# ScalarE's order in the step of a group's votes: q's scaling, slices and y's planes ahead of the first exponential

## The chip, the cores and the metric

The kernel runs on one core of a Trainium2 chip. The metric is the device time of one launch in microseconds; the time shown for the kernel before is the median of three runs. One more run was recorded by the hardware profiler, and all rows of the trace below come from that one. TensorE is PE here, VectorE DVE, ScalarE ACT, GpSimd POOL; SP is the engine that issues most DMAs.

## The reference

Attention over pooled keys, and then a mixture of experts that picks one expert for each row. Four batches, 12288 query rows each, 128 columns; 768 pooled keys per batch; 8 experts with 1024 hidden columns.

```python
kv_flat = kv.reshape(B, H//4, 4, W//4, 4, C).mean(axis=(2, 4)).reshape(B, -1, C) @ w_sr
k = v = kv_flat
a = softmax(q @ k.T / sqrt(C))            # per row, over 768 keys
x = a @ v                                 # 49152 rows of 128
logits = x @ w_gate                       # 8 experts
e = argmax(logits);  g = softmax(logits)[e]
y = g * (relu(x @ w1[e]) @ w2[e])
```

## The kernel before

The rows are taken in 96 blocks of 512 rows. A block is worked on in four chunks of 128 rows for its scores. fp32 products are made of three fp16 matmuls: every operand is cut into a high half and a low half (what the high half leaves), and high x high, high x low and low x high are summed. So each matmul operand costs one instruction that makes its high half and one that makes its low half.

The main loop has one step for each block t from 8 on. A step holds work of several blocks side by side:

- the scores of block t, chunk by chunk: six matmuls into a PSUM buffer `s` (there are two, used in turn), the row maximum on VectorE (L369, then L371 turns it into the bias `nmax`), the exponential on ScalarE into `a` (L376), its high half `ah[:, 0]` (chunks 0 and 2 on ScalarE, L399; chunks 1 and 3 on GpSimd, L397), its low half on GpSimd (L401), and a transposing DMA of both halves into `aT` (L402). `a`, `ah` and `nmax` have three buffers each, used in turn by the chunks;
- the product of `aT` with the values for block t-2 (18 matmuls into one PSUM bank `m`), its halves xh (ScalarE, L412) and xl (VectorE, L417), and its logits;
- the expert's two products for block t-8: eight slices f = 0 to 7, each three matmuls into a bank `m`, the slice's high half hh (ScalarE, L518) and low half hl (VectorE, L524), and then three matmuls into `y`. The second product runs three slices behind the first, so slices 5, 6 and 7 of a block go into `y` at the start of the next step. `y` has one PSUM buffer: slice 0 of the next block can go into it only when ScalarE has copied it out, as two planes of 16-bit halves (y's planes, `y_planes`, L547, two copies). There are three banks `m`, shared by the slices and the product with the values;
- block t+1's q: scaled on ScalarE (q_apply, L599), transposed on VectorE (q_turn, L603), high half on ScalarE (q_high, L607), low half on GpSimd (q_low, L612); the bound of block t+2's q on VectorE (q_max, L582). `q_scale` makes the unit that q_apply needs (L148, L149, L328);
- block t-9's output: planes joined and scaled on GpSimd (L553, L557), written by a DMA.

Four blocks form a group (two, in two places of the first batch). After a group's last block has its logits, the group votes on the expert that is computed for it; rows that chose another expert are done at the end. The votes take VectorE first: six small operations on the group's logits (`gate_part`, L445 to L453) around the end of one step, then in the next step the count (L674), a matmul of it beside chunk 1's scores, and the winner (L683 to L688). A step that follows such an end of step is the step of a group's votes; the change calls it `late`. `crowded(t)` tells the step before it. There are 23 late steps among the 88: 9, 12, 16, 20, 24, 26, and from 30 on every fourth, up to 94. In them q_scale has been run at the end of the step before. One step after the votes, the weights of the winner are cut into halves (`split_part`).

All of this order is written out by hand. `at(time, part, ...)` puts a part at a time of a nominal step of 18.7 us, the parts are sorted by their times, and the instructions are issued in that order; each engine then runs its own instructions strictly in the order of issue and waits where an operand isn't there. So the times only say what stands ahead of what on each engine, SP's DMA issues included. In the table of a chunk's times, the three numbers are the exponential, the high half, and the low half with its DMA.

Of the kernel before, what the change touches and what calls it, by code (L numbers as in the profile page):

```python
# [41 lines left out]
def attention_moe(ctx: ExitStack, tc, q, kv, w_sr, w_gate, w1, w2, out, tail=True):  # L42
# [17 lines left out]
    for b in range(B):  # L60
        at = [b * NB] + list(range(b * NB + (NBG if b else 2), (b + 1) * NB, NBG))
# [6 lines left out]
    LAG = NBG + 4  # L68
# [61 lines left out]
    def bank(start=0, end=0, ring=False):  # L130


        if "n" in EXPERTS and not ring:
            return EXPERTS["n"].tile([P, 512], F32, name="n")
        b = min(range(BANKS), key=lambda i: (free.get(i, 0), i))
        free[b] = end or max(free.values(), default=0) + 1
        return EXPERTS["m"].tile([P, 512], F32, name=f"m{b}")
# [515 lines left out]
    def block_logits(t, pl):  # L653
        BL[t]["pl"] = logits(BL[t]["x"], CH, pl)
# [310 lines left out]
    def done(t):  # L965
        return 0 <= t < NBLK
# [11 lines left out]
    def first_keys():  # L978

        for t in range(KT):  # L980
            kv_pool(0, t, raws.pop(t))
            pt = bank()[:, :P]
            k = KEYS[0]
            own = k.pop(("pooled", t))
            parts = k.pop(("parts", t))
            for i, part_ in enumerate(parts):
                mm(pt, part_, ident, i == 0, False)
            if t > 0:
                kv_project(0, t - 1, bank()[:, :P])
                kv_high(0, t - 1)  # L990
            mm(pt, own, ident, False, True)
            k["pt"] = pt
            kv_turned(0, t)
            if t > 0:
                kv_low(0, t - 1)
            if t == KT - 2:
                pq = bank()
                for c in range(CH):
                    nc.tensor.transpose(pq[:, c * P:(c + 1) * P], q0[:, c, :], ident)
                BL[0]["qhl"] = q_halves(pq, CH, nc.vector)  # L1000
        kv_project(0, KT - 1, bank()[:, :P])
        kv_high(0, KT - 1)
        kv_low(0, KT - 1)
# [7 lines left out]
    def closes(t):  # L1011

        return GRP[t] if done(t) and t == GROUPS[GRP[t]][-1] else None
# [21 lines left out]
    def at(time, part, *args):  # L1035
        heapq.heappush(events, (time, count[0], part, args))
        count[0] += 1

    def run(until):
        while events and events[0][0] < until:  # L1040
            _, _, part, args = heapq.heappop(events)
            part(*args)

    def beside(t, c, part, *args, where=0):
        OTHERS.setdefault((t, c), []).append((part, args, where))

    def begin(t):
        return FIRST + t * SHORT if t < LAG else t * LEN
# [76 lines left out]
    def plan_group(g, t):  # L1125

        if t < LAG:

            T = LAG * LEN
            group_gate(g)  # L1130
            at(begin(LAG - 1) + 4.64, gate_part, g)
            for _ in range(5):
                at(T + 3.5, gate_part, g)
            at(T + 6.1, group_count, g)
            beside(LAG, 2, group_votes, g)
            at(T + 11.4, group_first, g)
            at(T + 11.45, group_load, g)
            at(T + 12.35, gate_part, g)
            at(T + 12.4, group_left, g)
            at(T + 15.0, gate_part, g)  # L1140
            return plan_weights(g, t + 1, True)
# [14 lines left out]
        at(T + 7.25, group_left, g)  # L1156
        at(T + 15.0, gate_part, g)
        plan_weights(g, t + 1)

    def plan_weights(g, t, late=False):  # L1160
        T = t * LEN
        at(T + (18.9 if late else 17.1), scales_part, g)
        T += LEN
        at(T + (5.8 if late else 0.7), scales_part, g)
        beside(t + 1, 2 if late else 1, scales_part, g)
        at(T + (11.4 if late else 5.8), scales_part, g)
        at(T + 6.8, gate_part, g)
        at(T + 6.85, gate_part, g)
        at(T + (11.55 if late else 9.25), split_part, g, 0)
        at(T + 14.95, split_part, g, 0)  # L1170
        at(T + 16.8, split_part, g, 0)
        at(T + 18.9, split_part, g, 1)
        T += LEN
        at(T + 1.4, split_part, g, 1)
        at(T + 2.5, split_part, g, 1)
        at(T + 6.75, group_cover, g)
        at(T + 6.8, group_weight, g)
        at(T + 6.85, group_units, g)

    def crowded(t):  # L1180

        return t == LAG or closes(t - 2) is not None
# [50 lines left out]
    with tc.manual_schedule():  # L1233
        by_hand[0] = True
        first_keys()
        for t in range(LAG):
            plan_short(t)
            run(begin(t + 1) - 0.5)
        at(LAG * LEN + 2.9, lambda: block_logits(LAG - 3, bank(LAG * LEN + 2.9, LAG * LEN + 3.45)))
        at(LAG * LEN + 3.4, block_sum, LAG - 3)  # L1240
        plan_group(GRP[LAG - 3], LAG - 1)
        for i in range(4):
            at(begin(LAG + 3 + i) + 14.0, kv_keep, 0, i)
        at(LAG * LEN + 9.9, kv_keys_high, 0)
        at(LAG * LEN + 12.4, kv_keys_low, 0)
        at(LAG * LEN - 0.45, q_max, LAG + 1)
        beside(LAG, 0, q_bound, LAG + 1, where=1)
        for t in range(LAG, NBLK):
            m, z, T = t - LAG, t - 2, t * LEN
            job, last = jobs[m], jobs[m - 1] if m else None  # L1250
            job.update(n=BLK, w=G[GRP[m]]["w"])
            at(T + 17.15, lambda z=z, T=T: block_logits(z, bank(T + 17.15, T + 17.7)))
            if closes(z) is not None:
                plan_group(closes(z), t)
            for nb in range(1, B):
                plan_keys(nb, t)
            if t + 2 < NBLK:
                at(T + 0.2, q_load, t + 2, nc.sync)
                at(T + 7.35, q_max, t + 2)
                if crowded(t):  # L1260
                    at(T + 16.95, q_scale, t + 2)
                beside(t, 3, q_bound, t + 2, where=1)
            for c, time in enumerate((0.0, 3.65, 9.25, 14.85)):
                at(T + time, block_scores, t, c)
                at(T + time + 1.08, block_part, t, c)

            split = closes(t - 5) is not None
            for c, times in enumerate((
                    (2.36, 8.3, 9.15) if split else (2.36, 4.1, 4.95),
                    (7.2, 8.3, 9.2), (11.6, 12.72, 13.6), (17.2, 18.3, 19.15))):  # L1270
                for time in times:
                    at(T + time, block_part, t, c)
            at(T + 6.0, block_values, z, range(0, KT // 2), T + 6.0, T + 15.05)
            at(T + 11.6, block_values, z, range(KT // 2, KT))
            at(T + 13.6, block_high, z)
            at(T + 14.3, block_low, z)
            at(T + 17.45, block_sum, z)
            if t + 1 < NBLK:
                if t == LAG or not crowded(t - 1):
                    at(T + 2.25, q_scale, t + 1)  # L1280
                at(T + 4.95, q_apply, t + 1)
                at(T + 5.95, q_scale_scores, t + 1)
                at(T + 8.0, q_turn, t + 1)
                at(T + 9.3, q_high, t + 1)
                at(T + 10.8, q_low, t + 1, nc.gpsimd)
            for f, (time, high, low) in enumerate((
                    (1.05, 1.75, 2.4), (2.35, 3.45, 3.7), (4.7, 5.4, 6.05), (7.95, 8.6, 9.3),
                    (10.3, 11.0, 11.65), (13.55, 14.3, 15.05), (15.9, 16.6, 17.3), (17.4, 18.3, 18.5))):
                at(T + time, hidden_sum, job, f, T + time, T + low + 0.7)
                at(T + high, hidden_high, job, f)  # L1290
                at(T + low, hidden_low, job, f)
                if f >= DEEP:
                    at(T + time + 0.65, moe_second, job, f - DEEP)
                elif last:
                    at(T + time + 0.65, moe_second, last, NF - DEEP + f)
            if last:
                at(T + 6.02, planes, last)
                at(T + 15.3, block_join, m - 1, 0)
                at(T + 16.0, block_join, m - 1, 1)
                at(T + 16.85, block_out, m - 1)  # L1300
            run(T + LEN - 0.5)
        run(math.inf)
        by_hand[0] = False
# [85 lines left out]
```

## Time and profile before

| | us |
|---|---|
| median of three runs | 1906.08 (1905.27 to 1906.43) |
| profiled execution, its own time | 1902.9 |
| span of the profiled execution, first to last instruction | 1901.1 |

| engine | busy us | share of the span |
|---|---|---|
| PE | 1830.1 | 96% |
| DVE | 1490.6 | 78% |
| ACT | 1363.8 | 72% |
| POOL | 1347.7 | 71% |

The granted TensorE clock is 0.999 of full speed over the span. A row of the timeline gives the start in us from the first instruction, the duration in us, engine, line, operation, out<-in by the program's names, shapes, the count of instructions merged, and in brackets the engine's idle time before the row and what ended it. Engines overlap an instruction's end with the next one's start, so two in a row on ScalarE or VectorE start about 0.1 us closer than their durations. A matmul of 512 columns is shown with 0.38 us, but the next one starts 0.21 to 0.22 us after it.

### The profile page before, as it was taken

The numbers are of one execution on the slowest core, as the hardware profiler recorded it, in microseconds if no ns is written. First come the engines' busy times: TensorE is split into PE (matmuls) and PEld (weight loads), VectorE is DVE, ScalarE is ACT, GpSimd is POOL, SyncE is SP. The second block draws the span as 40 slices with busy tenths as digits, with TensorE's granted clock in tenths as the row PEclk, the third lists the DMA queues.
The fourth block names the chain that finished last, engine by engine and source line by source line (L and its number), as shares of the span: only waits on it lengthen the run. The fifth ranks groups of instructions, "written<-read, shape, count | busy, mean of one in ns | idle before, by whom it ended". The sixth has DMA issues, their size and how long they took to land.

```text
span 1901.1 us, 30989 instructions
## 1 busy us (share of the span) xinstructions
PE 1830.1 (96%) x9961; PEld 924.1 (49%) x9961; DVE 1490.6 (78%) x3167; ACT 1363.8 (72%) x2449; POOL 1347.7 (71%) x1387
## 2 busy tenths in 40 slices
PE   6899999999999999999999999999999999999997
PEld 5654444444444444444444444444444444444444
DVE  6787888888788787877787888878777777787595
ACT  3777767777777777768777778687776776776664
POOL 2778688677868777677687787676776776767453
PEclk9999999999999999999999999999999999999999
DMA  7988988767988886777779886877787678777452
GB/s 181 170 166 158 180 163 168 148 127 167 181 175 146 185 160 127 144 154 142 158 155 184 168 165 131 152 145 142 132 154 147 128 144 151 132 145 136 88 141 51
DMA packets 996565, 284.74 MB, mean 150 GB/s; under 512 B 900624, under 2 KB 980114, under 8 KB 996400
## 3 DMA queue, kind: packets, MB, share of 16 engines
q1 hardware_dynamic: 996272, 282.65, 76.0%
q8 instruction: 79, 1.29, 0.3%
q14 instruction: 86, 0.70, 0.1%
q0 software_dynamic: 128, 0.10, 0.0%
HBM read 80.42 MB, written 28.45 MB: 57 GB/s over the span
## 4 chain that ended last, share of the span: by engine, by line
PE 48%; DVE 23%; ACT 9%; POOL 6%; DMA 6%; issue 6%; SPq 1%; ACTq 0%; DVEq 0%; POOLq 0%
PE m L144 23%; PE y L144 14%; PE s L144 10%; DVE nmax L369 5%; DVE hl L524 5%; DMA aT<-ah 3%; ACT a L376 2%; POOL ah L401 2%; ACT ah L399 2%; DVE gate_d L449 2%; ACT hh L518 1%; DVE nmax L371 1%; DVE wm L471 1%; DVE xl L417 1%; DMA q_sb<-in_q_dram 1%
## 5 line engine op out<-in xcount | busy, mean ns | idle before, releaser
L401 POOL TENSOR_TENSOR ah<-a,ah 128x768 f16<-128x768 f32 x379 | 621.9, 1645 | 321.6 <-ACT ah L399 308.9
L524 DVE SCALAR_TENSOR_TENSOR hl<-m,hh 128x512 f16<-128x512 f32 (+1 forms) x784 | 526.7, 673 | 164.2 <-ACT hh L518 162.0
L518 ACT ACTIVATE hh<-m 128x512 f16<-128x512 f32 (+1 forms) x784 | 459.9, 588 | 230.9 <-PE m L144 229.7
L376 ACT ACTIVATE a<-s,nmax,qs 128x768 f32<-128x768 f32 x348 | 346.7, 996 | 176.7 <-DVE nmax L371 116.0
L144 PE MATMUL s<-k_sb,qh 128*128 128x384 f16 (+1 forms) x2316 | 447.7, 329 | 7.5 <-ACT a L376 6.9
L369 DVE TENSOR_REDUCE nmax<-s 128x1 f32<-128x768 f32 x386 | 366.2, 949 | 20.5 <-PE s L144 18.2
L144 PE MATMUL m<-aT,v_sb 128*128 128x512 f16 x1584 | 370.5, 379 | 1.5 <-DVE hl L524 1.5
L144 PE MATMUL y<-hh,w2h 128*128 128x512 f16 (+1 forms) x776 | 292.4, 377 | 27.0 <-ACT y L547 26.4
L144 PE MATMUL m<-xh,w1h 128*128 128x512 f16 (+1 forms) x776 | 292.2, 376 | 4.8 <-DVE hl L524 2.9
L144 PE MATMUL y<-hl,w2h 128*128 128x512 f16 (+1 forms) x776 | 292.7, 377 | 1.2 <-DVE hl L524 1.2
L144 PE MATMUL y<-hh,w2l 128*128 128x512 f16 (+1 forms) x776 | 292.7, 377 | 0.0
L144 PE MATMUL m<-xh,w1l 128*128 128x512 f16 (+1 forms) x776 | 292.5, 377 | 0.0
L144 PE MATMUL m<-xl,w1h 128*128 128x512 f16 (+1 forms) x776 | 292.4, 377 | 0.0
L144 PEld LDWEIGHTS <-qh 128*128 128x128 f16 x2100 | 204.1, 98 | 177.4 <-DVE qs L148 8.3
L144 PEld LDWEIGHTS <-v_sb 128*128 128x128 f16 x1764 | 169.7, 98 | 207.4 <-issue 10.0
L144 PEld LDWEIGHTS <-w2h 128*128 128x128 f16 x1552 | 150.8, 98 | 210.3 <-issue 33.9
L397 POOL CAST ah<-a 128x768 f16<-128x768 f32 x185 | 153.0, 827 | 89.2 <-ACT a L376 82.1
L144 PEld LDWEIGHTS <-w1h 128*128 128x128 f16 x1552 | 136.0, 97 | 119.1 <-issue 10.7
L399 ACT CAST ah<-a 128x768 f16<-128x768 f32 x194 | 161.7, 834 | 17.5 <-DMA aT<-ah 8.9
L417 DVE SCALAR_TENSOR_TENSOR xl<-m,xs,xh 128x512 f16<-128x512 f32 x88 | 66.1, 751 | 132.2 <-ACT xh L412 131.4
L553 POOL COPY o<-yT 128x512 uint16<-128x512 uint16 x190 | 136.7, 766 | 26.1 <-DMA yT<-y 25.8
L612 POOL TENSOR_TENSOR qh<-qT,qh 128x512 f16<-128x512 f32 (+1 forms) x95 | 111.1, 1170 | 48.8 <-ACT qh L607 48.7
(242 smaller groups left out, 2062.9 us busy)
## 6 DMA issues: line engine op xcount, KB each, us to landing
kv_raw<-in_moe_w_dram SPq DMA_DIRECT2D x54, 512.0 KB, 4.8
out_dram<-o SPq DMA_DIRECT2D x96, 256.0 KB, 2.5
q_sb<-in_q_dram SPq DMA_DIRECT2D x380, 64.0 KB, 2.6
kv_raw<-in_kv_dram SPq DMA_DIRECT2D x84, 256.0 KB, 4.7
aT<-ah SPq DMA_TRANSPOSE x379, 3.8
aT<-in_kv_dram SPq DMA_DIRECT2D x12, 256.0 KB, 6.7
k_dram<-k_sb SPq DMA_DIRECT2D x8, 192.0 KB, 2.6
v_dram<-v_sb SPq DMA_DIRECT2D x8, 192.0 KB, 2.6
```

The source lines that it names most:

```text
L144: return nc.tensor.matmul(o, l, r, start=start, stop=stop)
L369: nc.vector.tensor_reduce(nmax, pss[:, :, :KH], axis=AX.XY, op=ALU.max, negate=True)
L376: nc.scalar.activation(a.rearrange("p (h k) -> p h k", h=2), pss[:, :, :KH], AF.Exp, bias=nmax, scale=units[c] if units else 1.0, accum_ou ...
L397: nc.gpsimd.tensor_copy(ah[:, 0], a)
L399: nc.scalar.copy(ah[:, 0], a)
L401: nc.gpsimd.tensor_sub(ah[:, 1], a, ah[:, 0])
L417: nc.vector.scalar_tensor_tensor(xl[:, :n], po[:, :n], k["xs"][:, 0:1], xh[:, :n], op0=ALU.mult, op1=ALU.subtract)
L449: nc.vector.scalar_tensor_tensor(d2, d, 0.0, iota, op0=ALU.is_ge, op1=ALU.mult)
L518: nc.scalar.activation(hh[:, :n], ph[:, :n], AF.Relu)
L524: nc.vector.scalar_tensor_tensor(hl[:, :n], ph[:, :n], 0.0, hh[:, :n], op0=ALU.max, op1=ALU.subtract)
L553: nc.gpsimd.tensor_copy(o.bitcast(U16).rearrange("p c (d i) -> p i c d", i=2)[:, i], yT.rearrange("p (i c) d -> p i c d", i=2)[:, i])
L612: by.tensor_sub(ql, BL[t].pop("qT"), qh)
```

## The change

Two things in the main loop. In a late step, chunk 0's exponential, high half and low half go from 2.36, 4.1, 4.95 to 7.1, 9.35, 10.2; chunk 1's go from 7.2, 8.3, 9.2 to 9.25, 10.25, 11.3; and q's scaling (q_apply) goes from 4.95 to 1.9. On ScalarE the order of a late step was slice 0, exponential 0, slice 1, high half 0, q's scaling, slice 2, y's planes, exponential 1, slice 3, q's high half, slice 4. It becomes slice 0, q's scaling, slice 1, slice 2, y's planes, exponential 0, slice 3, exponential 1, q's high half, high half 0, slice 4. On GpSimd low half 0 moves behind the votes' three small operations, chunk 1's high half follows it, and q's low half comes between that and low half 1. On SP the transposing DMA of chunk 0 moves behind y's transposing DMA and the load of the winner's weights.

In step 9 alone (the first late step, whose weights are split in the same step) chunk 2's high and low half go from 12.72 and 13.6 to 14.35 and 15.2, which is behind xh, and the first operation of the split goes behind exponential 2.

```diff
-        at(T + (11.55 if late else 9.25), split_part, g, 0)
+        at(T + (11.65 if late else 9.25), split_part, g, 0)
...
-            split = closes(t - 5) is not None
-            for c, times in enumerate((
-                    (2.36, 8.3, 9.15) if split else (2.36, 4.1, 4.95),
-                    (7.2, 8.3, 9.2), (11.6, 12.72, 13.6), (17.2, 18.3, 19.15))):
+            late, split = t > LAG and crowded(t - 1), closes(t - 5) is not None
+            first, second = ((7.1, 9.35, 10.2), (9.25, 10.25, 11.3)) if late else (
+                (2.36, 8.3, 9.15) if split else (2.36, 4.1, 4.95), (7.2, 8.3, 9.2))
+            third = (11.6, 14.35, 15.2) if t == LAG + 1 else (11.6, 12.72, 13.6)
+            for c, times in enumerate((first, second, third, (17.2, 18.3, 19.15))):
                 for time in times:
                     at(T + time, block_part, t, c)
...
-                at(T + 4.95, q_apply, t + 1)
+                at(T + (1.9 if late else 4.95), q_apply, t + 1)
```

## Rows read from the trace of the kernel before

**Rows 1.** Waits of PE, steps 8 to 94: us in total, times, longest us.
```profile
PE y L144 <- ACT y L547: 24.6, 23, 1.4
...
PE m L144 <- DVE xl L417: 2.8, 3, 1.5
```

**Rows 2.** Windows of steps 77 and 78 (late): length, busy (count) PE, PEld, DVE, ACT, POOL.
```profile
1419.66:1438.03 18.37, 18.37 (x101) 9.02 (x100) 13.35 (x30) 13.11 (x24) 12.67 (x12) 1.00 0.77 146
1438.03:1457.76 19.73, 18.62 (x102) 9.04 (x101) 16.18 (x33) 12.78 (x25) 12.43 (x13) 1.00 0.74 149
```

**Rows 3.** Timeline of PE in late step 78, and the start of step 79.
```profile
1443.67 0.38 PE L144 MATMUL y<-hh,w2l 128*128 128x512 f16 x1
...
1446.32 0.38 PE L144 MATMUL m<-xh,w1l 128*128 128x512 f16 x1
1447.81 0.38 PE L144 MATMUL y<-hh,w2h 128*128 128x512 f16 x1 [1.11 <-ACT y L547]
...
1448.46 1.14 PE L144 MATMUL s<-k_sb,qh 128*128 128x384 f16 x6
...
1461.41 0.82 PE L144 MATMUL s<-k_sb,qh 128*128 128x384 f16 x4
```

**Rows 4.** Timeline of ACT in the same stretch.
```profile
1443.40 0.99 ACT L376 ACTIVATE a<-s,nmax,qs 128x768 f32<-128x768 f32 x1 [2.95 <-DVE nmax L371]
...
1444.38 0.59 ACT L518 ACTIVATE hh<-m 128x512 f16<-128x512 f32 x1
1444.86 0.83 ACT L399 CAST ah<-a 128x768 f16<-128x768 f32 x1
1445.58 0.73 ACT L599 ACTIVATE q_sb<-q_sb,qs 128x512 f32<-128x512 f32 x1
1446.21 0.59 ACT L518 ACTIVATE hh<-m 128x512 f16<-128x512 f32 x1
1446.68 1.08 ACT L547 COPY y<-y 128x512 uint16<-128x512 uint16 x2
...
1449.82 0.62 ACT L607 CAST qh<-qT 128x512 f16<-128x512 f32 x1 [0.56 <-DVE qT L603]
...
1453.43 0.68 ACT L412 ACTIVATE xh<-m,xs 128x512 f16<-128x512 f32 x1
...
1462.85 0.83 ACT L399 CAST ah<-a 128x768 f16<-128x768 f32 x1
```

**Rows 5.** Timeline of DVE in the same stretch.
```profile
1438.96 1.69 DVE L449 SCALAR_TENSOR_TENSOR gate_d<-gate_d,iota_e 128x128 f32<-128x128 f32 x1
...
1441.01 0.29 DVE L453 TENSOR_TENSOR gate_d<-gate,iota_e 128x128 f32<-128x128 f32 x1
...
1443.22 0.68 DVE L524 SCALAR_TENSOR_TENSOR hl<-m,hh 128x512 f16<-128x512 f32 x1
1445.00 0.69 DVE L524 SCALAR_TENSOR_TENSOR hl<-m,hh 128x512 f16<-128x512 f32 x1 [1.10 <-ACT hh L518]
...
1454.14 0.75 DVE L417 SCALAR_TENSOR_TENSOR xl<-m,xs,xh 128x512 f16<-128x512 f32 x1 [2.06 <-ACT xh L412]
...
1461.21 0.15 DVE L148 TENSOR_SCALAR qs<-s 128x1 f32<-128x1 f32 x1
```

**Rows 6.** Timeline of POOL in the same stretch.
```profile
1438.87 1.64 POOL L401 TENSOR_TENSOR ah<-a,ah 128x768 f16<-128x768 f32 x1
1445.77 1.64 POOL L401 TENSOR_TENSOR ah<-a,ah 128x768 f16<-128x768 f32 x1 [5.26 <-ACT ah L399]
...
1458.75 1.64 POOL L401 TENSOR_TENSOR ah<-a,ah 128x768 f16<-128x768 f32 x1
```

**Rows 7.** Line L149 by operation: ns min/median/max, first and last start us.
```profile
L149 DVE TENSOR_SCALAR qs<-qs x87: 153/154/157, 111.9 to 1736.6; 128x1 int32<-128x1 int32 x87
L149 DVE TENSOR_SCALAR ws<-ws x27: 157/526/531, 94.5 to 1858.1; 128x2 int32<-128x2 int32 x27
```

**Rows 8.** Line L402, the transposing DMAs of `ah`: issue to landing.
```profile
DMA to landing us min/median/max: 3.6/3.8/8.4
```

## The prediction, written before the change was run

> **What bounds the kernel now.** I read the waits of PE first, then the windows of single steps, then each engine's timeline in one late step. The windows show PE busy without a break in step 77 (18.37 of 18.37 us), while late step 78 takes 19.73 us with 18.62 of PE work [rows 2]. So PE sets the time, and a late step is where it stands still. The waits say for what: over the main loop PE waited 24.6 us, 23 times, for y's planes, once in each late step [rows 1]; the next entry of weight is 2.8 us for xl. PE's timeline shows the place: the first matmul of slice 0 into `y` starts at 1447.81 after 1.11 us of idling, the last of the slice's own matmuls having started at 1446.32 [rows 3].
>
> ScalarE's timeline shows why the planes are late. It stood idle for 2.95 us until 1443.40, waiting for chunk 0's `nmax`, with slice 1, q's scaling and slice 2 queued behind that exponential; the planes came at 1446.68 [rows 4], although the last matmul into `y` had started at 1443.67 [rows 3]. `nmax` itself is late because VectorE is: the votes' operations stand ahead of it.
>
> **The change part by part.** All times are those of step 78, and names of steps those of its neighbours. Matmuls of 512 columns start 0.22 us apart: three of them lie between 1447.81 and 1448.46 [rows 3].
>
> *ScalarE, first half of the step.* Nothing is added or removed, only the order changes. Slice 0 ended at 1440.45 (1443.40 less 2.95). Then q's scaling, 0.73, to 1441.2; its unit was made in the step before, so it waits for nothing of the votes. Slice 1, 0.59, to 1441.8. Slice 2's matmuls end three places before 1443.67, at 1443.02 + 0.38 = 1443.4, so slice 2 runs 1443.5 to 1444.0. The planes need the matmul at 1443.67 + 0.38 = 1444.05: 1.08 us, to 1445.2. Exponential 0 follows, 0.99, to 1446.2. All durations from [rows 4].
>
> *PE.* Slice 0 could enter `y` at 1446.32 + 0.22 = 1446.54, and the planes are out 1.3 us sooner, so the wait goes whole. It cost 1447.81 - 1446.54 = 1.27 us, 0.16 more than the 1.11 that the row calls idle. What is late next on PE: chunk 2's scores need the buffer that exponential 0 empties. They would start at 1448.46 - 1.27 = 1447.19, 1.0 us after that exponential; this cover is what exponential 0's new place leans on.
>
> *VectorE.* Slice 1's low half waited 1.10 us for ScalarE [rows 5]. Its high half is now there at 1441.8, so it starts one pitch (0.60, a duration of 0.68 less the overlap) after the row at 1443.22: at 1443.82 instead of 1445.00, 1.18 earlier. Behind it VectorE ran without a break up to the wait for xh: `nmax` 1, the winner of the votes, the unit, slice 2, q_max, q_turn, slice 3, `nmax` 2. All these come 1.18 earlier, and with them what ScalarE waits for: q's high half (it idled 0.56 for q_turn), at 1448.64. High half 0 now goes behind it, to 1450.0; slice 4 and exponential 2 follow with no new wait, since exponential 2 waits for `nmax` 2 anyway. xh moves from 1453.43 to about 1452.25, xl likewise, and VectorE's end of the step with it.
>
> *What comes back.* In step 79 chunk 1's scores start at 1461.41, 0.05 after the read of the bound at 1461.21 + 0.15 [rows 3, 5], which shares their buffer. VectorE brings that 1.18 earlier, PE could be there 1.27 earlier. So 0.09 us comes back and 1.18 stays.
>
> *GpSimd and SP.* Low half 0 waits until 1450.0 instead of 1445.77 [rows 6]. GpSimd's busy 12.43 us of the step [rows 2] less 1.64 and some 0.75 before 1445.77, plus the 2.63 after 1457.76 (1458.75 + 1.64 = 1460.39), less 0.7 for the votes' parts (0.75 and 0.7 are estimates) leave 12.0 us to do from 1450.0: to 1462.0, 5.5 us into a step 79 that now starts at 1456.5. It was 2.6 us into it before. Step 79's first low half needs ScalarE's cast at 1462.85 + 0.83 = 1463.68, 5.9 us in, so GpSimd has caught up by 0.4. q's low half, third in GpSimd's new order, ends near 1453.6, 2.9 us before the scores that read it. The transposed chunks are read two steps later, so a DMA 4 us later costs nothing there; on SP the weights' load no longer stands behind chunk 0's, which costs nothing either. Cost of this part: none, bounded above by the second and fourth rivals.
>
> *Step 9.* xl's longest wait, 1.5 us [rows 1], is there. Chunk 2's cast (pitch 0.72, from 1444.86 to 1445.58) leaves xh's way, and VectorE is 1.18 ahead: 1.9 us earlier against a PE that is 0.4 earlier. Between 0 and 1.5; I take 1.3, near the upper end, since 1.9 covers 1.5 and 0.4.
>
> *Sum.* 24.6 + 23 x 0.16 (3.7) - 22 x 0.09 (2.0; the late steps but 9) + 1.3 = 27.6 us. From the profiled execution's 1902.9 (a span of 1901.1 and 1.8 around it) that makes 1875.3; the runs' median lies 3.2 above that execution, so the same 27.6 from 1906.08 gives 1878.5.
>
> **The rivals.**
>
> *Half comes back.* On ScalarE exponential 0, slice 3, exponential 1, q's high half, high half 0 and slice 4 now follow each other closely. If they push exponential 2 and xh 0.6 us behind my times, xl, the end of VectorE's step and the read of the bound slip alike and PE pays in step 79. For it: the row at 1461.41 shows that PE has no slack there. Against: exponential 2 waits for `nmax` 2, not for ScalarE. 22 x 0.6 = 13 us back: 1892.
>
> *GpSimd holds VectorE up.* VectorE's 1.69 us at 1438.96 ends 0.14 after GpSimd's low half of 1438.87 to 1440.51, while an operation on the same shape takes 0.29 when GpSimd is idle [rows 5, 6]. Chunk 3's low half, now 3.8 to 5.4 us into step 79, meets L149's one-column operation there. Held to the end of the low half, it would put slice 0's low half 1.6 us back and the product with the values, which needs its bank, some 0.35: 22 x 0.35 = 8 us back, 1886. Against: 87 such instructions took 153 to 157 ns, none longer, while the two-column form was held to 526 [rows 7]. The Trainium skill has this rule (SBUF — State Buffer, "Who interferes with whom"): GpSimd and a VectorE instruction with two SBUF inputs, or of a kind with a two-port mode, such as `tensor_scalar`, lock each other out for a whole instruction. By that rule the trace agrees at 1438.96; for one column it does not.
>
> *Slower.* The next step's cast of chunk 0 (5.09 us in, 1462.85 less 1457.76) writes the `ah` buffer that chunk 1's DMA reads. That low half now ends near 1455.3; with a median landing of 3.8 us [rows 8] the buffer is free 2.6 us into step 79. With 8.4, the longest seen, it is free 7.2 in: ScalarE is 2.1 late. That step's planes end 2.9 us after the cast starts (1444.86 to 1446.68 + 1.08), so 8.0 in, and are needed 8.5 in (1446.54 less 1438.03): 1.6 us of it is paid, and 1.6 - 1.18 = 0.4 is lost each time: 1906 + 22 x 0.4 - 1.3 = 1914. It turns slower only where the landing takes over 8.0 us (3.8 + 2.5 + 0.5 + 1.2) in most late steps. Against: median 3.8.
>
> *It does not do what it says.* The wait at `y` goes, but VectorE keeps its lag, and all but 0.1 us comes back at 1461.41: about 1904. Against: the 1.10 us that VectorE waited for ScalarE.
>
> *More.* VectorE's lead also removes waits for low halves elsewhere in the loop, up to 0.3 us a late step: 1872.
>
> **How the numbers follow.** Forecast 0.70 (own range 1874 to 1885: each late step between 0.9 and 1.4 us), half back 0.10, GpSimd's hold 0.04, nothing 0.06, slower 0.05, more 0.05. Range 1871 to 1892: from "more" to "half back", with 0.11 left out. Faster by over 0.2% (3.8 us, about what a measurement of this kernel can tell from none): 0.70 + 0.10 + 0.04 + 0.05 = 0.89; within it 0.06; slower 0.05.
>
> **What would show it.** Right: PE's waits for y's planes fall from 24.6 us to near 0; step 78's counterpart lasts about 18.5 us; ScalarE's idle 2.95 is split into short waits for PE; slice 1's low half on VectorE follows slice 0's without 1.10 of idling; GpSimd's last low half ends some 5.5 us into the next step. Wrong: a new PE wait at chunk 2's scores on exponential 0; PE's wait at chunk 1's scores of the next step much above 0.1; ScalarE casts waiting for the DMA of `ah`; VectorE's short operations stretched beside GpSimd's low halves.

## The result, and the profile after

The changed kernel took 1884.43 us (median of four runs, 1881.83 to 1885.2) against 1906.26 for the kernel before (1905.27 to 1908.36): a ratio of 0.988, with a 95% interval of 0.9868 to 0.9892, which is 20.6 to 25.2 us. 1878.5 had been predicted, with a range of 1871 to 1892. The profiled execution of the changed kernel took 1881.8 us, with a span of 1880.1.

PE's waits in steps 8 to 94 answer to [rows 1] (us in total, times, longest us); these are all that the view lists. y's planes are gone from it, and xl's longest wait fell from 1.5 to 1.1 us.

```profile
PE m L144 <- DVE hl L524: 3.6, 16, 0.3
PE m L144 <- DVE xl L417: 1.9, 3, 1.1
PE m L144 <- POOL w1l L504: 1.1, 1, 1.1
PE s L144 <- DVE count L674: 0.7, 3, 0.3
PE s L144 <- DVE qm L582: 0.6, 1, 0.6
```

Windows of late step 78 and of step 79 (length; busy time and count of PE, PEld, DVE, ACT, POOL; granted clock): the late step took 19.73 us in [rows 2] and is now as long as PE's work in it.

```profile
1422.75:1441.20 18.45, 18.45 (x101) 9.03 (x100) 16.09 (x33) 12.89 (x24) 9.56 (x10) 1.00 0.64 144
1441.20:1459.78 18.58, 18.57 (x101) 8.97 (x100) 15.47 (x35) 13.86 (x26) 13.70 (x14) 1.00 0.85 153
```

ScalarE in the late step, beside [rows 4] (subtract 15.28 us from a time of before). The exponential no longer stands ahead of slice 1, and the 2.95 us of idling became waits for PE:

```profile
1424.57 0.60 ACT L518 ACTIVATE hh<-m 128x512 f16<-128x512 f32 x1 [1.47 <-PE m L144]
1425.07 0.71 ACT L599 ACTIVATE q_sb<-q_sb,qs 128x512 f32<-128x512 f32 x1
1425.87 0.60 ACT L518 ACTIVATE hh<-m 128x512 f16<-128x512 f32 x1
1428.22 0.60 ACT L518 ACTIVATE hh<-m 128x512 f16<-128x512 f32 x1 [1.76 <-PE m L144]
1428.81 1.07 ACT L547 COPY y<-y 128x512 uint16<-128x512 uint16 x2
1429.77 1.01 ACT L376 ACTIVATE a<-s,nmax,qs 128x768 f32<-128x768 f32 x1
...
1433.35 0.62 ACT L607 CAST qh<-qT 128x512 f16<-128x512 f32 x1 [0.26 <-DVE qT L603]
1433.87 0.83 ACT L399 CAST ah<-a 128x768 f16<-128x768 f32 x1
...
1436.95 0.68 ACT L412 ACTIVATE xh<-m,xs 128x512 f16<-128x512 f32 x1
```

VectorE, beside [rows 5]: the two slices' low halves follow each other without the 1.10 us, the gate's L455 takes 0.34, and L449 still takes 1.69.

```profile
1423.68 1.69 DVE L449 SCALAR_TENSOR_TENSOR gate_d<-gate_d,iota_e 128x128 f32<-128x128 f32 x1
...
1427.94 1.28 DVE L524 SCALAR_TENSOR_TENSOR hl<-m,hh 128x512 f16<-128x512 f32 x2
...
1431.76 0.34 DVE L455 SCALAR_TENSOR_TENSOR gate_d<-gate_d,xs,gate 128x128 f32<-128x128 f32 x1
```

GpSimd, beside [rows 6]: low half 0 starts 4.3 us later in the step, and the last low half that it owes ends at 1446.51, 5.3 us into step 79.

```profile
1434.78 1.65 POOL L401 TENSOR_TENSOR ah<-a,ah 128x768 f16<-128x768 f32 x1 [2.91 <-DVE nmax L369]
1436.37 0.83 POOL L397 CAST ah<-a 128x768 f16<-128x768 f32 x1
1437.15 1.16 POOL L612 TENSOR_TENSOR qh<-qT,qh 128x512 f16<-128x512 f32 x1
1438.28 3.25 POOL L401 TENSOR_TENSOR ah<-a,ah 128x768 f16<-128x768 f32 x2
...
1444.86 1.65 POOL L401 TENSOR_TENSOR ah<-a,ah 128x768 f16<-128x768 f32 x1
```

PE across the place of the old wait, beside [rows 3]: slice 0 enters `y` one pitch behind its neighbour, with no bracket.

```profile
1431.04 0.38 PE L144 MATMUL m<-xh,w1l 128*128 128x512 f16 x1
1431.26 0.38 PE L144 MATMUL y<-hh,w2h 128*128 128x512 f16 x1
...
1431.90 1.14 PE L144 MATMUL s<-k_sb,qh 128*128 128x384 f16 x6
...
1444.55 0.38 PE L144 MATMUL y<-hh,w2l 128*128 128x512 f16 x1
1444.94 1.15 PE L144 MATMUL s<-k_sb,qh 128*128 128x384 f16 x6
```

**Where the time went, step by step.** From the first score matmul of step 8 to that of step 95 the loop took 1648.7 us before and 1623.3 after: 25.4 less. The 23 late steps are 30.9 us shorter in sum (a typical one 1.27, step 9 2.47). The steps right behind them are 4.5 longer: +0.07 or 0.08 in the typical one, but +1.46 in step 10 and +0.3 to 0.7 in 17, 25, 43, 51, 59 and 67. The steps one further are 0.85 longer in sum, the rest 0.2. So 5.5 came back. Steps 25, 43 and 67 follow late steps that gained 1.53 to 1.63, more than the typical one.

**What lies outside the loop.** The changed kernel's step 8 began at 112.91 us instead of 108.86, in a stretch that the change doesn't touch. PE was 1.7 us behind already when it came to a wait for a key load; that took 2.21 us instead of 1.38, and PE was then granted half the clock. In order, a row of before, one of after, and the window in which after's clock is 0.50 (1.2 GHz, against 2.4 at 1.00):

```profile
25.59 2.04 PE L144 MATMUL m<-ident,kv_raw 128*128 128x128 f32 x16 [1.38 <-DMA kv_raw<-in_kv_dram]
```
```profile
28.12 3.32 PE L144 MATMUL m<-ident,kv_raw 128*128 128x128 f32 x16 [2.21 <-DMA kv_raw<-in_kv_dram]
```
```profile
30.00:32.00 2.00, 2.00 (x11) 2.00 (x10) 0.00 (x0) 0.10 (x1) 0.00 (x0) 0.50 0.57 91
```

The same 16 matmuls took 1.28 us more, and the kernel was 4.2 us behind by the next weights' product (28.56 before, 32.72 after). This start differs from run to run: step 8 began between 109.9 and 115.3 us in the profiles of the ten experiments. It is why loops, not spans, are compared below wherever a few us matter.

### The profile page after: what moved, and what is told of

It is laid out like the page before. It is cut to its first block, busy times and chain, and to the rows that moved or that the text cites. A ratio compares the mean times of both kernels' runs of the same rounds, so it can differ in the third digit from the quotient of the medians.

```text
span 1880.1 us, 31011 instructions
## 1 busy us (share of the span) xinstructions
PE 1831.2 (97%) x9961; PEld 926.0 (49%) x9961; DVE 1489.8 (79%) x3167; ACT 1366.8 (73%) x2449; POOL 1343.9 (71%) x1387
## 4 chain that ended last, share of the span: by engine, by line
PE 51%; DVE 24%; ACT 7%; DMA 7%; POOL 5%; issue 5%; SPq 1%; DVEq 0%; ACTq 0%; POOLq 0%
PE m L144 25%; PE y L144 15%; PE s L144 11%; DVE hl L524 6%; DVE nmax L369 5%; DMA aT<-ah 4%; POOL ah L401 2%; ACT ah L399 2%; ACT a L376 2%; DVE wm L471 1%; DVE xl L417 1%; DVE gate_d L449 1%; ACT hh L518 1%; DVE nmax L371 1%; DVE qT L603 1%
## 5 line engine op out<-in xcount | busy, mean ns | idle before, releaser
L397 POOL CAST ah<-a 128x768 f16<-128x768 f32 x185 | 153.4, 829 | 74.1 <-ACT a L376 69.2
```

What stands on the lines that cost most here:

```text
L397: nc.gpsimd.tensor_copy(ah[:, 0], a)
```

## The experiments

Loop times are those from step 8 to step 95, as above. The kernel before took 1908.3 to 1908.5 us beside these runs.

**1. Is q's scaling's new place needed?** The changed kernel with only that put back:

```diff
-                at(T + (1.9 if late else 4.95), q_apply, t + 1)
+                at(T + 4.95, q_apply, t + 1)
```

> The change with q's scaling back at its old place (4.95) in the late steps; chunk 0's exponential stays behind y's planes. Theory (only the exponential stood in the planes' way): q's scaling fits into ScalarE's idle time between slices 1 and 2, so nothing is lost: 1884 us, within 2 us of the changed kernel, and PE's waits for y's planes stay near 1.8 us (the two at the end of the run). Rival (each instruction that goes ahead of the exponential gives its own part): the 0.73 us of q's scaling come back in 23 late steps, up to 17 us: 1901.

Measured: 1882.8 us, ratio 0.9865 (0.985 to 0.988), loop 1625.7: the theory held. PE doesn't wait for y's planes in steps 8 to 94 here either, and there is no difference beyond some 2 us of the loop. What follows: the gain is in the exponential's place, not in q's.

**2. Is PE's wait alone the loss?** The kernel before with only q's scaling moved ahead, which brings y's planes out sooner and leaves slice 1 behind the exponential:

```diff
-                at(T + 4.95, q_apply, t + 1)
+                at(T + (1.9 if t > LAG and crowded(t - 1) else 4.95), q_apply, t + 1)
```

> The kernel before with q's scaling alone moved to 1.9 in the late steps. Theory: the planes still stand behind the late exponential, but one instruction of 0.63 us pitch less stands between them, so PE's wait at y falls from 1.11 to about 0.5 us per late step: 23 x 0.6 = 14 us, 1892. Rival (order of q's scaling does not matter while the exponential is ahead): 1905.

Measured: 1907.06 us, ratio 0.9993 (0.9982 to 1.0003). My theory missed. PE's wait at `y` fell from 24.6 to 11.2 us, and a typical late step became 0.61 us shorter, but the step behind it 0.58 to 0.61 longer; the loop is as long as before (1648.6). PE's waits, and late step 78 with its successor:

```profile
PE y L144 <- ACT y L547: 11.2, 21, 0.8
...
PE s L144 <- DVE qs L148: 3.3, 21, 0.2
...
PE m L144 <- DVE lg L430: 2.4, 9, 0.5
```
```profile
1445.02:1464.13 19.11, 18.61 (x101) 9.04 (x100) 15.56 (x32) 12.22 (x23) 11.82 (x13) 1.00 0.71 144
1464.13:1483.25 19.12, 18.73 (x102) 8.96 (x101) 16.02 (x35) 14.39 (x26) 11.61 (x11) 1.00 0.74 144
```

The wait moved to VectorE's results, the logits and the read of the bound. In step 79 the product behind chunk 0's scores, which waits for the logits, starts 0.40 us later in the step than before, and chunk 1's scores a further 0.2 later; together that is the 0.61. (The view lists less, since it counts as idle only what lies behind a matmul's modelled end.) VectorE's own row shows the lag that it kept, the same 1.10 us as in [rows 5]:

```profile
1451.99 0.69 DVE L524 SCALAR_TENSOR_TENSOR hl<-m,hh 128x512 f16<-128x512 f32 x1 [1.10 <-ACT hh L518]
```

**3. What is step 9 worth?** The change in the 22 late steps but 9, with step 9's order as before:

```diff
-        at(T + (11.65 if late else 9.25), split_part, g, 0)
+        at(T + (11.55 if late else 9.25), split_part, g, 0)
...
-            late, split = t > LAG and crowded(t - 1), closes(t - 5) is not None
+            late, split = t > LAG + 1 and crowded(t - 1), closes(t - 5) is not None
...
-            third = (11.6, 14.35, 15.2) if t == LAG + 1 else (11.6, 12.72, 13.6)
+            third = (11.6, 12.72, 13.6)
```

> The change in all late steps but step 9 (there everything as before, the split and chunk 2 too). In the two traces step 9 became 2.47 us shorter and step 10 1.46 us longer, where PE waited 1.14 us for GpSimd's low half of the expert's first weights. Theory: step 9's part of the change is worth the difference, 1.0 us: 1885.4. Rival (step 9's gain is whole and step 10's length is chance): 2.5 us lost, 1887.

Measured: 1887.8 us, ratio 0.9893 (0.9878 to 0.9908), loop 1627.3. The number is the rival's, but the steps don't bear the rival out. Steps 9 and 10 together are 2.5 us longer here than after the change: step 9 by 3.65, step 10 shorter by 1.1, so step 10's length in the changed kernel was not chance. More than the wait went into step 9, because PE idled 1.51 us for xl and was then granted 1.2 GHz (windows as above):

```profile
149.50:151.45 1.95, 0.44 (x3) 0.10 (x1) 0.80 (x2) 1.95 (x4) 1.34 (x1) 1.00 0.00 0
...
152.50:153.50 1.00, 1.00 (x4) 0.36 (x3) 0.96 (x3) 0.42 (x2) 1.00 (x2) 0.50 0.85 119
153.50:154.60 1.10, 1.10 (x4) 0.37 (x3) 0.34 (x2) 1.10 (x3) 1.10 (x2) 0.50 1.45 28
```

In this stretch 512-column matmuls started 0.43 us apart instead of 0.215. The kernel before had the same wait without that fall, so step 9 was 1.18 us shorter there. Against that step 9 the change is worth the 1.0 us of the theory. The loop is 4.0 us longer than after the change; the other 1.5 lie in other steps and are not explained here.

**4. Does GpSimd's lateness give the 5.5 us back?** The changed kernel with high and low half 0 earlier, ahead of chunk 1's exponential on ScalarE and so sooner on GpSimd:

```diff
-            first, second = ((7.1, 9.35, 10.2), (9.25, 10.25, 11.3)) if late else (
+            first, second = ((7.1, 8.4, 9.0), (9.25, 10.25, 11.3)) if late else (
```

> The change with chunk 0's high half at 8.4 and its low half at 9.0 in the late steps: on ScalarE directly behind exponential 0, ahead of slice 3, so GpSimd gets low half 0 some 2.5 us sooner and its later halves with it. Theory (what the change gave back after the late steps, 4.5 us in the next steps and 0.9 in those behind, hangs on GpSimd's lateness through the ah buffers and step 10's weights): those steps fall back by 3 to 5 us in sum, 1880. Rival (it hangs on the DMA queue alone, the weights' and keys' loads ahead of the transposes): 1884, the same steps as long as in the changed kernel. Slice 3 is 0.1 to 0.2 us later on ScalarE, which costs nothing by both.

Measured: 1878.4 us, ratio 0.984 (0.9827 to 0.9854), loop 1620.9. The steps right behind the late ones give back 1.9 us instead of 4.5; those one further are 1.2 longer than in the kernel before (0.9 after the change). So the theory held in kind, with 2.2 us in sum where 3 to 5 were expected, and the loop is 2.4 shorter; the rest of the 6 us between the medians lies outside the loop or between runs. The 1.4 us of steps 17, 51 and 59 went (in each PE had waited 0.2 or 0.3 us for a slice's low half). Step 10 is still 1.12 longer than before, and 25, 43 and 67 have their 0.34 or 0.35 still.

**5. The rest of it: loads ahead of a transposing DMA on SP.** Experiment 4 with the next batch's key loads issued just behind chunk 3's transposing DMA instead of just ahead of it:

```diff
-                at(T + 0.3, lambda u=u: raws.update({u: kv_load(nb, u)}))
+                at(T + 0.5, lambda u=u: raws.update({u: kv_load(nb, u)}))
```

> The run with chunk 0's high half at 8.4, and besides, the keys' loads at 0.5 instead of 0.3, so that on SP chunk 3's transposing DMA of the step before is issued ahead of them. Theory (what is left of the give-back in the steps with a load is the wait of ScalarE's chunk 2 cast for that DMA): ScalarE's waits for the DMA of ah in the main loop go, 0.5 to 2 us less than 1878.4. Rival (the DMAs land late for another reason, or the loads, now later, stall the folding): 1878 to 1880.

Measured: 1876.5 us, ratio 0.9835 (0.9822 to 0.9849), loop 1618.3: as the theory had it. The steps right behind a late one give back 1.5 us in sum, and those one further are 1.31 shorter than in the kernel before. ScalarE's waits say why (after the change, in experiment 4, then here). These are casts that write `ah`, and the first entry is the wait until a DMA has read it. For the second the profile shows no releaser; that it is the same wait is inferred from its going with the first:

```profile
ACT ah L399 <- DMA aT<-ah: 9.8, 8, 2.3
...
ACT ah L399 <- issue: 8.7, 5, 2.5
```
```profile
ACT ah L399 <- DMA aT<-ah: 8.5, 5, 2.5
...
ACT ah L399 <- issue: 7.2, 3, 2.5
```
```profile
ACT ah L399 <- DMA aT<-ah: 2.3, 1, 2.3
```

Against experiment 4 alone the time is not told apart (the intervals overlap); the waits are.

**6. Must the planes go ahead of the exponential?** The changed kernel with the exponential right behind slice 1, which still lifts VectorE's 1.10 us, and with low half 0 early:

```diff
-            first, second = ((7.1, 9.35, 10.2), (9.25, 10.25, 11.3)) if late else (
+            first, second = ((3.47, 7.0, 7.05), (7.2, 8.3, 9.2)) if late else (
```

> The changed kernel, but in the late steps exponential 0 comes directly behind slice 1 (3.47), so slice 2 and y's planes stand behind it as they did before; chunk 0's high half at 7.0, behind the planes, low half 7.05, chunk 1 as before the change (7.2, 8.3, 9.2). Theory after the run that moved q's scaling alone (what lasts is VectorE's lead: slice 1's low half no longer waits 1.1 us for its high half; the planes, 0.7 us later than in the changed kernel, are still out 0.6 us before they are needed): late steps 1.27 us shorter as in the changed kernel, and GpSimd has low half 0 early, so 1878 to 1880. Rival (the planes have to go ahead of the exponential): PE waits at y again, 0.5 us or more in 23 steps, 1890 or above.

Measured: 1904.97 us, ratio 0.998 (0.9971 to 0.9989). The theory missed by 25 us. A late step gained 0.97 us and the step behind it lost 0.92. PE didn't wait at `y`; VectorE was late again, for another reason. The largest wait of PE, then two rows, VectorE's and GpSimd's, and line L455 over the run (ns min/median/max):

```profile
PE m L144 <- DVE lg L430: 10.3, 21, 0.5
```
```profile
1449.39 1.49 DVE L455 SCALAR_TENSOR_TENSOR gate_d<-gate_d,xs,gate 128x128 f32<-128x128 f32 x1
```
```profile
1449.09 1.65 POOL L401 TENSOR_TENSOR ah<-a,ah 128x768 f16<-128x768 f32 x1 [6.23 <-ACT ah L399]
```
```profile
L455 DVE SCALAR_TENSOR_TENSOR gate_d<-gate_d,xs,gate x27: 208/1492/1498, 88.8 to 1884.8; 128x128 f32<-128x128 f32 x23, 128x64 f32<-128x64 f32 x2, 128x8 f32<-128x8 f32 x2
```

L455 started 0.30 us behind GpSimd's low half 0 and ended 0.14 behind it: held for 1.15 us of its 1.49. In the kernel before and after the change the two don't meet, and it takes 0.34.

**7. The same, with low half 0 out of L455's way.** Experiment 6 with one number changed, 7.05 to 8.4, which moves low half 0 with its DMA (the cut is against the changed kernel):

```diff
-            first, second = ((3.47, 7.0, 7.05), (7.2, 8.3, 9.2)) if late else (
+            first, second = ((3.47, 7.0, 8.4), (7.2, 8.3, 9.2)) if late else (
```

> The run with exponential 0 directly behind slice 1, and of it only chunk 0's low half moved, from 7.05 to 8.4: on GpSimd behind the votes' three operations and chunk 1's high half. ScalarE's order is that run's. Theory (that run lost VectorE's lead at L455, which GpSimd's low half 0 held from 0.34 to 1.49 us; the planes' place behind the exponential costs nothing): L455 is back at 0.34, the late steps keep their 1.27 us and the steps after them give back 0.1 instead of 0.9: 1878 to 1882. Rival (the planes have to go ahead, or the exponential's new place itself holds VectorE up): 1900 to 1905 with L455 at 0.34.

Measured: 1880.33 us, ratio 0.9849 (0.9834 to 0.9864), loop 1621.4, L455's median back at 342 ns. The theory held. Between experiments 6 and 7 lie 24.6 us of the medians and 23.1 of the loops (1644.5 and 1621.4): the price of one instruction on GpSimd that stands beside one on VectorE in each late step. And the planes need not go ahead of the exponential.

**8. The hold that was there all along.** L449 takes 1.69 us beside chunk 3's low half in [rows 5, 6]. Experiment 4, and in the steps ahead of the late ones chunk 3's high half made by ScalarE, with its low half late enough to miss the gate's operations:

```diff
-        if c % 2:
+        if c % 2 and pool:
             nc.gpsimd.tensor_copy(ah[:, 0], a)
...
-            for c, times in enumerate((first, second, third, (17.2, 18.3, 19.15))):
+            fourth = (17.2, LEN + 3.48, LEN + 3.49) if votes_next(t) else (17.2, 18.3, 19.15)
+            for c, times in enumerate((first, second, third, fourth)):
```

Here `votes_next(t)` is `LAG < t < NBLK - 1 and crowded(t)`, and `pool` is false for chunk 3 of such a step.

> The run with chunk 0's high half at 8.4, and besides, in the step before each late step (but step 8) chunk 3's high half is made by ScalarE instead of GpSimd, in the late step's idle time behind slice 1, and its low half follows there. So GpSimd is idle while VectorE does the votes' operations on 128x128 (L447, L449). Theory (the lock: those two take 0.75 and 1.69 us because GpSimd reads SBUF then, and 0.29 beside an idle GpSimd): they take 0.3 us each, VectorE comes into the late step 1.8 us sooner, the waits for the count and for slice 0's low half go, and the 0.1 to 0.2 us that comes back per late step too: 5 to 8 us less than 1878.4, 1871 to 1874. Rival (they are that long by themselves, from their operands): both as long as before, 1878 to 1880.

Measured: 1869.3 us, ratio 0.9799 (0.9786 to 0.9812), a little more than expected. L447 and L449 take 0.29 us each (0.75 and 1.69 after the change), so the rival, that they are long by themselves, falls. GpSimd's low half starts 3.7 us behind the two, and late step 78 takes 18.40 us:

```profile
1410.60 0.29 DVE L447 TENSOR_TENSOR gate_d<-lg,gate 128x128 f32<-128x128 f32 x1
1410.93 0.29 DVE L449 SCALAR_TENSOR_TENSOR gate_d<-gate_d,iota_e 128x128 f32<-128x128 f32 x1
```
```profile
1414.97 1.64 POOL L401 TENSOR_TENSOR ah<-a,ah 128x768 f16<-128x768 f32 x1 [5.18 <-ACT ah L399]
```
```profile
1410.45:1428.85 18.40, 18.40 (x101) 9.05 (x100) 14.94 (x33) 14.13 (x26) 11.64 (x13) 1.00 0.77 162
```

**9. Would that alone have been enough?** The kernel before with only this edit of experiment 8 (and `pool` as there):

```diff
-                    (7.2, 8.3, 9.2), (11.6, 12.72, 13.6), (17.2, 18.3, 19.15))):
+                    (7.2, 8.3, 9.2), (11.6, 12.72, 13.6),
+                    (17.2, LEN + 3.48, LEN + 3.49) if votes_next(t) else (17.2, 18.3, 19.15))):
```

> The kernel before the change, and of all that only chunk 3's high half on ScalarE in the steps before the late ones, made in the late step behind slice 1, its low half with it. ScalarE's order in the late step is otherwise the old one. Theory (the late exponential was late because GpSimd held VectorE's L447 and L449 up by 1.8 us): the exponential comes 1.8 us sooner, the planes about 1.1 sooner (the cast adds 0.7 ahead of them), PE's wait at y falls from 1.27 to 0.2 us and VectorE leads as well: 1880 to 1885. Rival (the order on ScalarE is what costs, whatever VectorE's lag): at most half the change's gain, 1895 to 1905.

Measured: 1894.07 us, ratio 0.9932 (0.9917 to 0.9946). Neither figure was met in full. PE's wait at `y` fell to 6.0 us, in 8 steps, but L455 was now held (median 923 ns), and the steps behind the late ones lost 6.7 us. In the loop this edit is worth 16.6 us alone and 9.0 on top of experiment 4: part of what it frees is the same lag.

```profile
PE y L144 <- ACT y L547: 6.0, 8, 1.1
```

**10. All of it.** Experiment 8 with the key loads of experiment 5.

```diff
-                at(T + 0.3, lambda u=u: raws.update({u: kv_load(nb, u)}))
+                at(T + 0.5, lambda u=u: raws.update({u: kv_load(nb, u)}))
```

> The run with chunk 3's high half on ScalarE, and the keys' loads at 0.5 as well: both gains in one kernel. Theory (they act in different places, VectorE at the votes and the DMA queue in steps with a load): 1.5 to 2.5 us less than 1869.3, 1867 to 1868. Rival (the first has already given the steps with a load their slack): 1869 to 1870.

Measured: 1866.38 us, ratio 0.9783 (0.9769 to 0.9796), loop 1609.5: the fastest of all, 18 us below the changed kernel. That is nearer to the theory than to the rival: the loop is 2.4 us shorter than experiment 8's, though the intervals of the two overlap. The view lists three waits of PE in steps 8 to 94:

```profile
PE m L144 <- DVE xl L417: 1.1, 1, 1.1
PE m L144 <- DVE hl L524: 0.5, 1, 0.5
PE m L144 <- POOL w1l L504: 0.4, 1, 0.4
```

## Why the prediction was right, step by step

- *ScalarE's new order: right.* Less 15.28 us, the prediction had slice 0 end at 1425.17, the planes start at 1428.8, q's high half at 1433.36 and xh at 1436.97; the rows have slice 0 end at 1425.17 (1424.57 + 0.60), the planes start at 1428.81, q's high half at 1433.35 and xh at 1436.95. With xh on time, the rival "half comes back" (xh 0.6 us behind) falls.
- *PE: right.* Its wait at `y` went whole, chunk 2's scores start three pitches behind with no wait for exponential 0, and a typical late step gained 1.27 us as worked out.
- *VectorE brings the next step's bound as much earlier as PE comes: right, and the condition for everything.* Chunk 1's scores of step 79 are 0.17 us late, and that step 0.07 us longer (0.09 forecast). Experiment 2 shows the counter-case: it takes more than half of PE's wait at `y` away and leaves VectorE's 1.10, and all is given back. That is the rival "it does not do what it says", for another edit. Experiment 7 shows what is enough: with slice 1 and q's scaling ahead of the exponential and the planes still behind it, a typical late step gains the same 1.27 us. So the planes' place ahead of the exponential, by which the prediction had the wait at `y` go, isn't what the gain needs.
- *Step 9's 1.3 us: right for step 9 (2.47 in all, 1.27 + 1.3 forecast), wrong for the pair with step 10.* Step 10 gave 1.46 back; PE waited 1.14 us there for the low half of the new weights, which GpSimd makes.
- *GpSimd and SP "cost none": this is the term that failed, with most of the 3.5 us that came back beyond the forecast.* Its lateness was forecast well (5.5 us into the next step, 5.3 measured), but not who pays: the low half of the weights in step 10, and in a few steps ScalarE's cast of a chunk, behind an `ah` that a late DMA still reads, whose wait rose from 12.8 us in all (five and three times) to 18.5 (eight and five). That is the mechanism of the "slower" rival at a small part of its price, on chunk 2's cast instead of chunk 0's, in steps with loads on SP; experiments 4 and 5 take most of it away. Not all of the 3.5 us is GpSimd's: in steps 25, 43 and 67 the 0.34 us each stay in experiments 4 and 5 and go only in 8 (these steps are then 0.10 shorter than before). There chunk 1's scores are 0.19 us later in the step, so it is in part the term that stood at 0.09. In sum 5.5 us came back where 2.0 stood, against late steps that gained 30.9 where 29.6 stood: 25.4 for 27.6.
- *The rest of the distance to 1884.43.* 1906.26 less 25.4 and 0.3 more at the end would be 1881.2; the medians differ by 21.8 only, with 25.2 the upper end of the interval. In the two profiled executions the account closes: 25.4 less 4.1 at the start and 0.3 at the end is 21.1, by which they differ (1902.9 and 1881.8). Starts between 109 and 115 us are large enough for the medians too; which starts the runs without a trace had isn't known.
- *GpSimd holds VectorE up: priced at the wrong place.* L149 on one column was not held, as [rows 7] had said: after the change it ran at 1444.92 for 0.15 us, inside the low half of 1444.86 to 1446.51. What can be held is L455, 1.15 us in experiment 6. That the change keeps clear of this is luck: it moves low half 0 from ahead of L455 to behind it, and the prediction didn't look at L455. Experiments 6 and 7 differ in that place alone, by 1.35 us of the nominal step, and the earlier one loses nearly the whole gain. L447 and L449 are held in both kernels; the prediction saw the 1.69 us and didn't ask what lifting them would give, which was another 9 us (experiment 8). The Trainium skill (SBUF — State Buffer, "Who interferes with whom") says that a VectorE instruction with two SBUF inputs and a GpSimd instruction that reads SBUF share a port, and that the one issued first has it to its end. The trace agrees for L447, L449 and L455, with 0.29, 0.29 and 0.34 us where no long instruction of GpSimd runs beside them, 0.75 for L447 behind chunk 3's high half (L397), and 1.69 and 1.49 for the other two behind a low half. Of `tensor_scalar` the same section says only that it can contend, when its operands meet the conditions of a two-port mode; the prediction left that condition out, so the 0.15 us of L149 doesn't speak against the section.

Left open: what part of the some 2 us between experiment 1's loop and the changed kernel's is chance, and what makes up the rest of the 0.34 us in steps 25, 43 and 67.

## What to carry to other kernels

Before taking a wait off the engine that sets the time, find the engine that brings the next thing that it will need; if that one doesn't gain as much in the same place, the wait only moves into the next step. In an order written by hand, list beside each GpSimd instruction what VectorE runs at that moment: a short VectorE operation can take four to six times as long there (0.34 and 1.49 us, 0.29 and 1.69), and moving either by a microsecond can be worth as much as the change that is tried. An engine that isn't the bound still pays for being made late, in the few steps that carry extra work, so these are to be worked out one by one.

## What was not expected of the hardware

- One operation of 0.34 us, held for 1.15 us in 18 of the 23 late steps and for less in four, cost 23.1 us of the loop (experiments 6 and 7), about its whole hold each time, on an engine that is busy for 79% of the span.
- PE's granted clock fell to 1.2 GHz after some waits and not after others alike: 1.51 us for xl in experiment 3 (matmuls then 0.43 us apart for some 2.5 us), but not after the same wait in the kernel before; after 1.92 us at 42.01 in the changed kernel, but not after the 1.92 us at 37.84 in the kernel before. No run here shows what tells them apart.
- The stretch ahead of step 8, the same in all twelve kernels, took from 108.9 to 115.3 us in their profiles: 6.4 us, nearly as wide as the spread of the fifteen runs of the kernel before beside experiments 1 to 4 (1903.45 to 1911.0).
